# A fused window-attention and gated-conv-FFN kernel: order and PSUM banks from a table, late conv taps on GpSimd and ScalarE, one batch's k transposed by DMA

## The chip, the core and the metric

The kernel runs on one core of a Trainium2 chip. A core has TensorE (PE in the profile: matmuls, with PEld for weight loads), VectorE (DVE), ScalarE (ACT), GpSimd (POOL) and SyncE (SP). SP issues DMAs here and computes nothing. Each engine works through its own list of instructions in order and waits on semaphores for the others. The metric is the device time of one execution in microseconds (us); lower is better.

## What is computed

The reference does attention in a window of 32 positions to either side, then an FFN whose hidden layer is gated by a convolution of 3 taps along the sequence. All inputs and the output are float32.

```python
def _attn_ref(q, k, v):
    B, H, S, D = q.shape                      # 8, 8, 576, 64
    scores = np.matmul(q, k.transpose(0, 1, 3, 2)) / np.sqrt(D)
    mask = np.abs(pos[:, None] - pos[None, :]) <= 32
    scores = np.where(mask, scores, -1000000000.0)
    attn = softmax(scores)
    return np.matmul(attn, v)

def _moe_ref(x, w_in, conv_w, w_out):         # x: (8, 576, 512), d_ff 1024, 3 taps
    h = np.maximum(x @ w_in, 0.0)
    conv_out = sum(conv_w[k] * hp[:, k:k + S, :] for k in range(3))   # hp: h padded by one row
    gate = 1.0 / (1.0 + np.exp(-conv_out))
    return h * gate @ w_out
```

## The kernel before

**Units of work.** Attention runs batch by batch (8), each in two halves of 288 rows (`s` = 0, 1). The FFN runs over the rows of all batches in 12 chunks of 384 (`CH`), so three chunks cover two batches. The first two chunks are cut in two pieces each, so that they can start before a whole batch is there. Within a chunk the hidden width of 1024 is 8 blocks `m` of 128.

**Attention of one half** (`attention`, line 640). `load_qk` (L391) and `load_v` (L422) have SP issue DMAs into float32 staging tiles. `cast_qk`, `cast_v` and `shift_v` turn them into bf16 through the helper `copy` (L301 on ACT, L303 on POOL, L307 on DVE); `shift_v` makes a second copy of v, `vo`, shifted by 64 rows. For batch 0 some of the casts may go to ACT or POOL, later ones go to POOL. `transposes` turns q and k by matmuls with the identity (L491) into PSUM; ACT or DVE copies the result to `qT` and `kT`. `scores` (L541) does the products of 64 rows with 128 keys, exp on ACT (L554) and the mask product (L565; DVE for batches 0 and 1, POOL after that, DVE for the last tile of 64 rows). `values` (L586) multiplies with v and a column of ones; DVE takes the reciprocal (L605) and scales into `xn` (L608). `turn` transposes `xn` into `xT`: by PE (L630) and a copy for batches 0 and 1, by a DMA transpose on SP (L621) for the others.

**FFN of one chunk** (`hidden`, line 662, and `project`, line 788). For each block `m`, four matmuls (L720) give the hidden layer, and ACT writes relu of half of it to `hT` (L736). The convolution is done in PSUM: PE adds a tap by multiplying with a diagonal matrix of the tap's weights (L751), DVE adds a tap by a scalar_tensor_tensor on the bank (L768). The planner's `taps` says which. For chunks 0 and 1 all three taps are PE's; for chunks 2 to 11 they are

```python
        return (1,) if m in TIMES["light"] else (0, 2)     # taps of PE; "light": (1, 2, 3, 7)
```

so that four blocks have one tap on PE and two on DVE, and four have two on PE and one on DVE. Then ACT takes tanh of the bank (L772) and DVE multiplies (1 + tanh) by the hidden value into `gT` (L775). `project` adds 8 matmuls of 512 columns per 128 rows (L795), ACT copies the result to `y_sb` (L806) and SP stores it (L809).

**Weights.** `load_w` brings w_in and w_out in two halves each through the staging tiles `wst`. `conv_weights` builds the 24 diagonals on DVE (L377).

**Order.** None of these calls emits an instruction at once. Each calls `add(on, prio, run, ...)`, which makes an `Op` with the engines it may run on and a cost for each, its due time `prio`, what it reads and writes, and the PSUM bank it takes (`alloc`). Operations are numbered in the order of these calls. `Plan.place` (line 122) is a list scheduler on the host: it keeps the time at which each engine and bank is free, and takes again and again, for the engine that can start first, the ready operation with the earliest due time. It also chooses the engine, where there is a choice, and the bank (one of 8, or a pair). The constants in `TIMES` set due times and how far the planner may reach ahead. At the end the operations are sorted by planned start, warm-up matmuls (`spin`, L817) are put into planned gaps of PE in the first 36 us, and the instructions are emitted in that order. Each engine's order and SP's order of DMAs are therefore fixed when the kernel is built.

The softmax here doesn't subtract the row's maximum and nothing guards it: scores larger than these inputs give would overflow.

## Time and profile before

| | before |
|---|---|
| time, median of 6 executions | 231.18 us (230.91 to 232.88) |
| the profiled execution: time, span | 232.16 us, 230.4 us |
| granted TensorE clock, mean | 0.993 |
| PE busy, matmuls | 213.1 us (92%), 2519 |
| DVE busy | 190.3 us (83%), 416 instructions |
| ACT busy | 171.2 us (74%), 350 |
| POOL busy | 158.1 us (69%), 160 |
| moved by DMA | 45.92 MB, mean 199 GB/s |

A busy time is the time in which an instruction of that engine was in flight, overlaps counted once. Instructions of one engine overlap by their start-up, so the price of one in a packed row is less than its mean duration. A group's row gives line, engine, operation, tiles and shapes, count, then busy time and mean ns of one, then how long the engine stood idle ahead of it and for whom. The slices cut the span in 40 equal parts and give the busy share in tenths (9 is 90% or more). The chain of waits is followed back from the last instruction through what released each step.

### The profile page before, as it was taken

To read this page: it belongs to the slowest core of one execution; us is meant where nothing else is said; L and a number is where in the kernel's file an instruction comes from. 1 tells how busy PE (TensorE), PEld (TensorE's weight loads), DVE (VectorE), ACT (ScalarE), POOL (GpSimd) and SP (SyncE) were. 2 spreads that over 40 slices of the span, in tenths; PEclk is the share of its full clock that TensorE was granted. 3 is DMA by queue.
4 is the path that set the end of the run, shared out by engine and by line. 5 is a ranking of instruction groups with operands and counts; after the bars stand their busy time and mean duration, and the time that the engine had idled before them with its cause. 6 is when DMAs were issued, how large, how long until landed. Compare 5 with 4: busy or idle time off the path is not lost.

```text
span 230.4 us, 6559 instructions
## 1 busy us (share of the span) xinstructions
PE 213.1 (92%) x2519; PEld 130.8 (57%) x2519; DVE 190.3 (83%) x416; ACT 171.2 (74%) x350; POOL 158.1 (69%) x160
## 2 busy tenths in 40 slices
PE   3686999999999997999999988999999999999992
...
DVE  6967467965989889988899977999898988998780
ACT  2384799968576987786988894878878893867642
POOL 6588895989999999986799939886999270000000
...
GB/s 177 289 263 273 278 254 298 327 233 317 279 175 289 101 286 187 267 170 136 251 311 151 270 158 299 137 215 192 291 230 130 127 38 71 91 91 47 89 48 137
DMA packets 68883, 45.92 MB, mean 199 GB/s; under 512 B 53980, under 2 KB 54004, under 8 KB 68852
## 3 DMA queue, kind: packets, MB, share of 16 engines
...
q8 instruction: 19, 0.31, 0.6%
...
q10 hardware_dynamic: 36, 0.01, 0.0%
HBM read 32.52 MB, written 9.44 MB: 182 GB/s over the span
## 4 chain that ended last, share of the span: by engine, by line
PE 64%; POOL 13%; DMA 13%; DVE 3%; SPq 2%; issue 1%; ACT 1%; ACTq 0%; POOLq 0%; DVEq 0%
PE ps_all L720 21%; PE ps_all L795 21%; PE ps_all L751 8%; DMA vst<-in_v_dram 6%; PE ps_all L586 5%; PE ps_all L491 4%; POOL vo L303 4%; DMA wst<-in_moe_w_out_dram 4%; DMA kst<-in_k_dram 3%; PE ps_all L541 3%; POOL attn L565 3%; POOL ve L303 3%; SPq L391 2%; POOL kn L303 2%; POOL qn L303 2%
## 5 line engine op out<-in xcount | busy, mean ns | idle before, releaser
L720 PE MATMUL ps_all<-xT,w_in_sb 128*128 128x385 bf16 (+4 forms) x448 | 77.1, 304 | 0.4 <-DVE xT L307 0.3
L768 DVE SCALAR_TENSOR_TENSOR ps_all<-hT,conv_w_sb,ps_all 128x384 f32<-128x384 bf16 x120 | 70.7, 614 | 6.8 <-PE ps_all L751 5.8
L795 PE MATMUL ps_all<-w_out_sb,gT 128*128 128x512 bf16 x288 | 67.4, 379 | 0.0
L772 ACT ACTIVATE ps_all<-ps_all 128x384 f32<-128x384 f32 (+3 forms) x112 | 49.0, 451 | 13.6 <-DVE ps_all L768 12.4
L775 DVE SCALAR_TENSOR_TENSOR gT<-ps_all,hT 128x384 bf16<-128x384 f32 (+3 forms) x112 | 52.6, 490 | 7.2 <-ACT ps_all L772 5.8
L565 POOL TENSOR_TENSOR attn<-attn,mask 128x1024 bf16<-128x1024 bf16 x24 | 50.9, 2138 | 10.8 <-ACT attn L554 10.7
L736 ACT ACTIVATE hT<-ps_all 128x385 bf16<-128x385 f32 (+4 forms) x112 | 48.6, 462 | 12.0 <-PE ps_all L720 11.1
L720 PEld LDWEIGHTS <-w_in_sb 128*128 128x128 bf16 x448 | 40.5, 98 | 20.6 <-POOL vo L303 0.9
L795 PEld LDWEIGHTS <-gT 128*128 128x128 bf16 x288 | 27.6, 98 | 29.6 <-issue 0.2
L751 PE MATMUL ps_all<-hT,diag_w 128*128 128x384 bf16 (+3 forms) x216 | 43.3, 291 | 0.4 <-DVE gT L775 0.3
L554 ACT ACTIVATE attn<-ps_all 128x1024 bf16<-128x1024 f32 (+1 forms) x40 | 36.4, 950 | 1.1 <-PE ps_all L541 0.5
L303 POOL TENSOR_SCALAR vo<-vst 64x1024 bf16<-64x1024 f32 (+1 forms) x36 | 35.1, 975 | 2.9
L806 ACT COPY y<-ps_all 128x512 f32<-128x512 f32 x36 | 21.1, 593 | 15.5 <-PE ps_all L795 11.4
L608 DVE TENSOR_TENSOR xn<-ps_all,rec 128x256 bf16<-128x256 f32 (+1 forms) x64 | 27.8, 479 | 0.3
L303 POOL TENSOR_SCALAR ve<-vst 128x512 bf16<-128x512 f32 (+1 forms) x41 | 25.5, 631 | 3.3 <-DMA vst<-in_v_dram 2.5
L303 POOL TENSOR_SCALAR kn<-kst 128x1152 bf16<-128x1152 f32 (+1 forms) x20 | 19.7, 987 | 7.8 <-DMA kst<-in_k_dram 7.5
L751 PEld LDWEIGHTS <-diag_w 128*128 128x128 bf16 x216 | 18.1, 97 | 8.0 <-DVE gT L775 0.7
L303 POOL TENSOR_SCALAR qn<-qst 128x1152 bf16<-128x1152 f32 (+1 forms) x20 | 19.3, 967 | 2.5 <-DMA qst<-in_q_dram 1.5
L586 PEld LDWEIGHTS <-attn 128*64 128x64 bf16 x640 | 12.6, 111 | 12.0 <-issue 6.1
L586 PE MATMUL ps_all<-ve,attn 128*64 128x65 bf16 x384 | 15.9, 198 | 2.3 <-DVE attn L565 1.2
L301 ACT COPY qT<-ps_all 128x640 bf16<-128x640 bf16 (+1 forms) x20 | 14.9, 758 | 2.8 <-PE ps_all L491 2.7
L565 DVE TENSOR_TENSOR attn<-attn,mask 128x1024 bf16<-128x1024 bf16 (+1 forms) x16 | 14.4, 918 | 2.7 <-ACT attn L554 2.6
...
## 6 DMA issues: line engine op xcount, KB each, us to landing
...
xT<-xn SPq DMA_TRANSPOSE x30, 3.3
```

Of the source, the lines that this page charges most:

```text
L303: nc.gpsimd.tensor_scalar(out=out_, in0=in_, scalar1=1.0, scalar2=0.0, op0=ALU.mult, op1=ALU.add)
L554: add(act(2 * w), t + 0.1, lambda e: nc.scalar.activation(at, ps(sl, 0, 1024).rearrange("p (e x) -> p e x", e=2)[:, :, 0:w], AF.Exp, bias= ...
L565: lambda e: ENG[e].tensor_tensor(out=x_, in0=x_, in1=m_, op=ALU.mult),
L586: nc.tensor.matmul(ps(sl, lo, lo + D + 1, 64 * j, 64 * j + 64), attn[a][:, 512 * h_ + col:512 * h_ + col + 64], (vo if tt % 2 else ve)[i][ ...
L608: add(dve(2 * n * D), t + 0.1, lambda e, y=y: nc.vector.tensor_tensor(out=xn[i][:, cs[0]:cs[0] + n].rearrange("p c (e g) d -> p c e g d", ...
L720: nc.tensor.matmul(ps(sl, 0, n), w_in_sb[:, kc, m * 128:(m + 1) * 128], x_[:, kc, a0:a1], start=(kc == 0), stop=(kc == KC - 1),)
L736: nc.scalar.activation(o_, i_, AF.Relu, bias=0.0, scale=0.5)
L751: nc.tensor.matmul(ps(sl, 0, no), diag_w[:, kk, m, :], hview(m, o0, o1, kk - 1), start=(kk == ks[0]), stop=(kk == ks[-1]),)
L768: add(("DVE", no / 960.0 + 0.13), tt + 0.1, lambda e, m=m, kk=kk, pv=pv: nc.vector.scalar_tensor_tensor(out=pv(), in0=hview(m, o0, o1, kk ...
L772: add(act(no), tt + 0.2, lambda e, sl=sl: nc.scalar.activation(ps(sl, 0, no), ps(sl, 0, no), AF.Tanh, bias=0.0, scale=1.0), writes=[sl], s ...
L775: add(dve(no), tt + 0.3, lambda e, m=m, mid=mid, i2=i2, pv=pv: nc.vector.scalar_tensor_tensor(out=gT[ig][:, m, o0:o1].rearrange("p (i x) - ...
L795: nc.tensor.matmul(ps(sl, 0, d_model), gT[ig][:, m, 128 * i:128 * i + 128], w_out_sb[:, m, :], start=(m == 0), stop=(m == MB - 1),)
```

## The change

- `Plan.place` no longer searches. `ORDER` lists all 1528 operations by number, `PICK` gives the engine of those that have a choice, `BANKS` the first bank of each operation that takes one, in order. A simple pass still computes planned starts from them.
- `taps` now gives four lists: taps of PE, ACT, DVE and POOL. There are five kinds of block, and the table `kinds` gives each block `m` one, with a row for chunks 2 to 8 and another for chunks 9 to 11. An ACT tap is an activation Copy with the tap's weight as a [128, 1] scale, written to the bank. POOL taps go to the float32 tile `tmp`; a second or third one is added by a POOL tensor_tensor. In kind 3 tanh reads `tmp`; in kind 4 DVE adds `tmp` to the bank.
- k of batch 6 (`"turned": ((6, 1),)`) is no longer loaded in the packed form and transposed by PE: the new `turned` loads it in five blocks of up to 128 rows, casts them on POOL and issues five DMA transposes on SP.
- All casts of batch 0 and of w_in may go to DVE as well (`both`), and batch 0's masks to POOL.
- The last 128 rows are projected in two halves of 256 columns; the second is copied by DVE, and each half has its own store.
- The numbers in `TIMES` are others; with the order taken from the table they have no part in it, apart from the tables named above.

```diff
+ORDER = [
+    73, 80, 0, 1, 2, 25, 17, 3, 10, 21, 26, 15, 29, 36, 27, 34, 30, 37, 47, 48, 20, 8, 51, 52, 28,
+    35, 45, 49, 4, 50, 74, 81, 91, 33, 32, 43, 39, 18, 24, 12, 9, 46, 53, 56, 31, 38, 54, 55, 19,
+    16, 57, 58, 44, 42, 41, 59, 60, 62, 63, 64, 66, 5, 14, 13, 61, 71, 78, 72, 79, 93, 92, 89, 90,
+    94, 95, 96, 97, 98, 65, 69, 67, 100, 70, 103, 104, 125, 129, 126, 40, 6, 128, 68, 239, 235, 101,
+    127, 120, 121, 23, 227, 105, 22, 124, 233, 234, 241, 122, 123, 231, 237, 228, 243, 229, 99, 76,
...
+    1521, 1522, 1523, 1517, 1518, 1519, 1524, 1525, 1526, 1527,
+]
+PICK = {
+    34: "POOL", 35: "POOL", 36: "POOL", 37: "DVE", 38: "DVE", 39: "DVE", 40: "POOL", 41: "ACT",
+    42: "POOL", 43: "POOL", 44: "POOL", 46: "ACT", 48: "ACT", 50: "DVE", 52: "DVE", 55: "DVE",
+    58: "DVE", 68: "DVE", 70: "ACT", 78: "ACT", 79: "ACT", 80: "POOL", 81: "ACT", 82: "DVE",
+    83: "DVE", 84: "DVE", 85: "POOL", 86: "POOL", 87: "POOL", 88: "POOL", 90: "ACT", 92: "ACT",
+    94: "DVE", 96: "ACT", 99: "DVE", 102: "DVE", 105: "DVE", 115: "ACT", 117: "DVE", 119: "DVE",
+    121: "DVE", 122: "POOL", 123: "POOL", 124: "POOL", 126: "POOL", 127: "ACT", 128: "POOL",
...
+BANKS = [
+    3, 0, 3, 0, 3, 4, 0, 2, 0, 2, 6, 5, 4, 4, 0, 6, 2, 4, 6, 0, 5, 4, 1, 3, 2, 5, 4, 0, 1, 6, 4, 5,
...
-    "light": (1, 2, 3, 7),
+    "kinds": ((2, 2, 4, 3, 2, 4, 0, 1), (1, 2, 0, 2, 0, 0, 2, 2), (3, 1, 4, 2, 3, 2, 2, 1)),
+    "turns": (2, 9),
+    "turned": ((6, 1),),
...
+        order, banks = [self.ops[i] for i in ORDER], iter(BANKS)
+        assert sorted(ORDER) == list(range(len(self.ops)))
+        for op in order:
+            e = op.eng = PICK.get(op.idx) or next(iter(op.on))
+            r = max([d.end for d in op.deps], default=0.0)
+            if op.alloc is not None:
+                n = op.alloc.n
+                x = next(banks)
+                r = max(bank[x:x + n] + [r])
+                assert r < 1e9, "no bank is free"
+                op.alloc.base = x
+                bank[x:x + n] = [1e9] * n
+            f = free[e]
+            if e == "PE":
+                f += self.SWITCH * (op.mode != mode)
+                mode = op.mode
+                r += self.LATE * (r > f)
+            op.start = max(r, f)
+            f = free[e] = op.start + op.on[e]
...
+    def both(n):
+
+        return ("DVE", n / 1920.0 + 0.2)
...
-        on = dict([act(n), pool(n)]) if (b, s) == (0, 0) else pool(n)
+        on = dict([act(n), pool(n), both(n)]) if b == 0 else pool(n)
...
-        on = dict([act(n), pool(n)]) if b == 0 and p1 <= 128 and c < 3 and p0 < 64 else pool(n)
+        on = dict([act(n), pool(n), both(n)]) if b == 0 else pool(n)
...
+    def turned(b, y, s):
+
+        i = b % NLD
+        src = (q, k)[y][b]
+        a0, a1, a2 = TIMES["ahead_t"]
+        for c in ((0, 1, 2), (3, 4))[s]:
+            t = when(b, s, 0.0) + 0.1 * c + 0.01 * y
+            p = min(128, S - 128 * c)
+            st_ = wst[y].rearrange("p (c h d) -> p c h d", c=4, h=H)[:, c] if c < 4 else rest[64 * y:64 * y + 64]
+            to = n2[y][:, c] if c < 4 else n2r
+            nk = ("n2", y, c) if c < 4 else "n2r"
+            key = ("rest", y) if c == 4 else ("wst", y, c)
+            add(sp(1.1), t - a0, lambda e, c=c, p=p, st_=st_: nc.sync.dma_start(
+                st_[0:p], src[:, 128 * c:128 * c + p, :].rearrange("h p d -> p h d")
+            ), writes=[key], dma=0.0112 * p, rel=t - a0)
+            add(pool(H * D), t - a1, lambda e, p=p, st_=st_, to=to: copy(
+                e, to[0:p].rearrange("p g e d -> p e g d"), st_[0:p].rearrange("p (e g) d -> p e g d", e=2)
+            ), reads=[key], writes=[nk])
+            lo = 128 * c + PAD * y
+            add(sp(1.26), t - a2, lambda e, p=p, lo=lo, to=to: nc.sync.dma_start_transpose(
+                out=(qT, kT)[y][i][:, :, lo:lo + p], in_=to[0:p].rearrange("p g e d -> p (g e d)")
+            ), reads=[nk], writes=[("Tc", y, i, c)], dma=0.0051 * p)
+
...
+            if (b, y) in TIMES["turned"]:
+                continue
...
+    KINDS = (
+        ((0, 2), (), (1,), ()), ((1,), (), (0, 2), ()), ((), (1,), (0, 2), ()), ((), (), (), (1, 0, 2)),
+        ((1,), (), (), (0, 2)),
+    )
+
     def taps(c, m):

         if c < 2:
-            return TIMES["taps"][c]
-        return (1,) if m in TIMES["light"] else (0, 2)
+            return TIMES["taps"][c], (), tuple(k_ for k_ in range(3) if k_ not in TIMES["taps"][c]), ()
+        return KINDS[TIMES["kinds"][(c >= TIMES["turns"][0]) + (c >= TIMES["turns"][1])][m]]
...
+            by_pe, by_act, by_dve, by_pool = taps(c, m)
+
+            def mm(e, m=m, sl=sl, ks=by_pe):
                 for kk in ks:
                     nc.tensor.matmul(
                         ps(sl, 0, no), diag_w[:, kk, m, :], hview(m, o0, o1, kk - 1),
                     )

             tt = t + (m + TIMES["lag"][0]) * dt
-            add(pe(no, len(taps(c, m))), tt, mm, reads=hk + [("diag", kk, m) for kk in taps(c, m)], writes=[sl], alloc=sl,
-                slots=[sl], group=gr)
+            if by_pe:
+                add(pe(no, len(by_pe)), tt, mm, reads=hk + [("diag", kk, m) for kk in by_pe], writes=[sl],
+                    alloc=sl, slots=[sl], group=gr)
             mid = hview(m, o0, o1, 0)
             i2 = mid.shape[1]

             def pv(sl=sl, i2=i2):
                 return ps(sl, 0, no).rearrange("p (i x) -> p i x", i=i2)

-            for kk in (0, 1, 2):
-                if kk in taps(c, m):
-                    continue
+            for kk in by_act:
+                add(("ACT", 0.000833 * no + 0.18), tt, lambda e, m=m, kk=kk, pv=pv: nc.scalar.activation(
+                    pv(), hview(m, o0, o1, kk - 1), AF.Copy, bias=0.0, scale=conv_w_sb[:, kk, m:m + 1],
+                ), reads=hk + ["conv_w"], writes=[sl], alloc=sl, slots=[sl], group=gr)
+            if by_pool:
+                r = NTM[0] % len(tmp)
+                NTM[0] += 1
+
+                def tv(x=0, r=r, i2=i2):
+                    return tmp[r][:, x, 0:no].rearrange("p (i x) -> p i x", i=i2)
+
+            for n_, kk in enumerate(by_pool):
+                add(pool(no), tt + 0.05, lambda e, m=m, kk=kk, tv=tv, n_=n_: nc.gpsimd.tensor_scalar(
+                    out=tv(n_ > 0), in0=hview(m, o0, o1, kk - 1), scalar1=conv_w_sb[:, kk, m:m + 1], scalar2=0.0,
+                    op0=ALU.mult, op1=ALU.add,
+                ), reads=hk + ["conv_w"], writes=[("tmp", r, n_ > 0)])
+                if n_:
+                    add(("POOL", 0.0021 * no + 0.155), tt + 0.05, lambda e, tv=tv: nc.gpsimd.tensor_tensor(
+                        out=tv(), in0=tv(), in1=tv(1), op=ALU.add,
+                    ), reads=[("tmp", r, True)], writes=[("tmp", r, False)])
+            if by_pool and by_pe:
+                add(("DVE", no / 960.0 + 0.13), tt + 0.1, lambda e, pv=pv, tv=tv: nc.vector.scalar_tensor_tensor(
+                    out=pv(), in0=tv(), scalar=1.0, in1=pv(), op0=ALU.mult, op1=ALU.add,
+                ), reads=[("tmp", r, False)], writes=[sl], slots=[sl], group=gr)
+            for kk in by_dve:
                 add(("DVE", no / 960.0 + 0.13), tt + 0.1, lambda e, m=m, kk=kk, pv=pv: nc.vector.scalar_tensor_tensor(
                     out=pv(), in0=hview(m, o0, o1, kk - 1), scalar=conv_w_sb[:, kk, m:m + 1], in1=pv(),
                     op0=ALU.mult, op1=ALU.add,
                 ), reads=hk + ["conv_w"], writes=[sl], slots=[sl], group=gr)
-            add(act(no), tt + 0.2, lambda e, sl=sl: nc.scalar.activation(
-                ps(sl, 0, no), ps(sl, 0, no), AF.Tanh, bias=0.0, scale=1.0
-            ), writes=[sl], slots=[sl], group=gr)
+            if by_pool and not by_pe:
+                add(act(no), tt + 0.2, lambda e, pv=pv, tv=tv: nc.scalar.activation(
+                    pv(), tv(), AF.Tanh, bias=0.0, scale=1.0
+                ), reads=[("tmp", r, False)], writes=[sl], alloc=sl, slots=[sl], group=gr)
+            else:
+                add(act(no), tt + 0.2, lambda e, sl=sl: nc.scalar.activation(
+                    ps(sl, 0, no), ps(sl, 0, no), AF.Tanh, bias=0.0, scale=1.0
+                ), writes=[sl], slots=[sl], group=gr)
...
-        for m0, m1 in ((0, 6), (6, MB)) if c == NCH - 1 else ((0, MB),):
-            def mm(e, m0=m0, m1=m1):
-                for m in range(m0, m1):
-                    nc.tensor.matmul(
-                        ps(sl, 0, d_model), gT[ig][:, m, 128 * i:128 * i + 128], w_out_sb[:, m, :],
-                        start=(m == 0), stop=(m == MB - 1),
-                    )
-
-            add(pe(d_model, m1 - m0), t + m0, mm,
-                reads=[("gT", ig, m, (i, x)) for m in range(m0, m1) for x in (False, True)]
-                + [("w_out", m) for m in range(m0, m1)],
-                writes=[sl], alloc=None if m0 else sl, slots=[sl], group=gr if m1 == MB else None)
         r = NYY[0] % NY
         NYY[0] += 1
-        add(act(d_model), t + 0.1, lambda e: nc.scalar.copy(out=y_sb[r], in_=ps(sl, 0, d_model)),
-            reads=[sl], writes=[("y", r)], slots=[sl], group=gr)
         r0 = c * CH + 128 * i
-        add(sp(), t + 0.2, lambda e: nc.sync.dma_start(out_rows[r0:r0 + 128, :], y_sb[r]),
-            reads=[("y", r)], dma=0.8)
+        end = c == NCH - 1 and i == 2
+        for f0, f1 in ((0, d_model // 2), (d_model // 2, d_model)) if end else ((0, d_model),):
+            for m0, m1 in ((0, 6), (6, MB)) if c == NCH - 1 else ((0, MB),):
+                def mm(e, m0=m0, m1=m1, f0=f0, f1=f1):
+                    for m in range(m0, m1):
+                        nc.tensor.matmul(
+                            ps(sl, f0, f1), gT[ig][:, m, 128 * i:128 * i + 128], w_out_sb[:, m, f0:f1],
+                            start=(m == 0), stop=(m == MB - 1),
+                        )
+
+                add(pe(f1 - f0, m1 - m0), t + m0, mm,
+                    reads=[("gT", ig, m, (i, x)) for m in range(m0, m1) for x in (False, True)]
+                    + [("w_out", m) for m in range(m0, m1)] + [(sl, 0)] * (f0 > 0),
+                    writes=[(sl, f0)], alloc=None if m0 or f0 else sl, slots=[sl],
+                    group=gr if m1 == MB and not end else None)
+            on = act(f1 - f0)
+            if end and f0:
+                on = dve(f1 - f0)
+            add(on, t + 0.1, lambda e, f0=f0, f1=f1: copy(e, y_sb[r][:, f0:f1], ps(sl, f0, f1)),
+                reads=[(sl, f0)], writes=[("y", r, f0)], slots=[sl], group=None if end else gr)
+            add(sp(), t + 0.2, lambda e, f0=f0, f1=f1: nc.sync.dma_start(
+                out_rows[r0:r0 + 128, f0:f1], y_sb[r][:, f0:f1]
+            ), reads=[("y", r, f0)], dma=0.8 * (f1 - f0) / d_model)
```

## The prediction

> **What bounds the kernel now.** I read the page's busy shares first, then its slices, then the busy time by stage, then the chain of waits in one stage, then the groups.
>
> The page, busy times and slices:
>
> ```profile
> PE 213.1 (92%) x2519; PEld 130.8 (57%) x2519; DVE 190.3 (83%) x416; ACT 171.2 (74%) x350; POOL 158.1 (69%) x160
> ...
> PE   3686999999999997999999988999999999999992
> ...
> DVE  6967467965989889988899977999898988998780
> ACT  2384799968576987786988894878878893867642
> POOL 6588895989999999986799939886999270000000
> ```
>
> PE is full from the fifth slice to the last but one; POOL is busy up to 80% of the span and then does nothing. Busy time by stage (columns: length, PE, PEld, DVE, ACT, POOL with their counts, clock, DMA share, GB/s):
>
> ```profile
> 0.00:40.00 40.00, 31.20 (x443) 23.05 (x443) 28.50 (x85) 26.77 (x64) 29.25 (x48) 0.96 1.00 262
> ...
> 65.00:182.00 117.00, 113.62 (x1368) 66.66 (x1366) 104.74 (x215) 94.14 (x180) 101.16 (x86) 1.00 0.88 209
> 182.00:226.00 44.00, 44.00 (x316) 23.27 (x313) 37.64 (x73) 30.21 (x64) 4.20 (x2) 1.00 0.21 70
> ...
> 150.00:160.00 10.00, 10.00 (x124) 5.78 (x123) 9.71 (x21) 7.77 (x17) 8.09 (x7) 1.00 0.84 223
> ```
>
> From 65 to 182 us chunks 2 to 8 run beside the attention of batches 2 to 7; from 182 to 226 us it is chunks 9 to 11. PE has 157.6 of these 161 us. The chain of waits from 100 to 125 us is PE alone, and its pieces give PE's true prices (a matmul's own mean of 327 ns is mostly pipeline):
>
> ```profile
> by line: PE ps_all L795 35.0%; PE ps_all L720 32.7%; PE ps_all L751 12.4%; PE ps_all L491 8.5%; PE ps_all L586 6.5%; PE ps_all L541 5.5%
> ...
> 105.04 0.78 PE ps_all L491 x14
> ...
> 109.65 0.33 PE ps_all L751 x2
> 110.96 1.73 PE ps_all L795 x8
> ```
>
> So a tap (one diagonal matmul of the conv, L751, 384 columns) costs 0.163 us, a transpose (L491) 0.056. Prices of the others, from the groups by shape:
>
> ```profile
> L768 DVE SCALAR_TENSOR_TENSOR ps_all<-hT,conv_w_sb,ps_all 128x384 f32<-128x384 bf16 x120 | 70.7, 614 | 6.8 <-PE ps_all L751 5.8
> L565 POOL TENSOR_TENSOR attn<-attn,mask 128x1024 bf16<-128x1024 bf16 x24 | 50.9, 2138 | 10.8 <-ACT attn L554 10.7
> ...
> L772 ACT ACTIVATE ps_all<-ps_all 128x384 f32<-128x384 f32 x80 | 39.0, 494 | 13.1 <-DVE ps_all L768 12.4
> ...
> L303 POOL TENSOR_SCALAR ve<-vst 128x512 bf16<-128x512 f32 x39 | 24.3, 632 | 3.3 <-DMA vst<-in_v_dram 2.5 <-POOL vo L303 0.3
> ```
>
> **The conv, part by part.** Before, chunks 2 to 11 have 12 taps on PE and 12 on DVE each. The row of `kinds` for chunks 2 to 8 has three blocks of kind 0 (PE 2, DVE 1), one of kind 1 (PE 1, DVE 2), four of kind 2 (ACT 1, DVE 2): PE 7, DVE 13, ACT 4. For chunks 9 to 11: PE 3, DVE 10 and one add, ACT 3, POOL 8 taps and 5 sums.
> - PE: 7x5 + 3x9 = 62 taps less, 62 x 0.163 = 10.1 us, all on the path.
> - DVE: 7x1 - 3x1 = 4 more, at 70.7/120 = 0.59: +2.4 us.
> - ACT: 37 taps. The nearest row is the tanh of the same size: 494 ns, and two in a row take 0.86 (195.73 us), so 0.38 each when packed: 14.1 us. That tanh has immediate operands; these taps read their scale from a [128,1] column, which no ACT instruction of this trace does. The Trainium skill (ScalarE: Activation LUTs, "What ACT_TABLE_LOAD costs") says such an operand adds about 93 ns: 0.47 each, 17.5 us by estimate. This speaks against the change by 3.4 us of ACT. I take 17.5; ACT is not the largest, so the sum moves by nothing, but every tap stands that much later before its DVE taps.
> - POOL: from 632 ns at 512 and about 1180 at 1152 elements, a 384-element tap is 0.52; a sum of two tensors lies between 0.80 (2138 x 384/1024) and 2.14, taken as 0.9. 24 x 0.52 + 15 x 0.9 = 26 us, where POOL has 4.2 of 44 us: hidden, unless a block's chain (3 taps, 2 sums, 3.4 us) starts late. The table puts them behind batch 7's last mask, and PE still has chunk 8's projections and chunk 10's hidden layer (10 us) meanwhile. Without that cover the price is the 3.4 us, once. DVE's taps read one SBUF operand and last 614 ns both beside a busy POOL (90 to 170 us) and an idle one (615 after 187 us), so I charge no contention.
>
> **Order and banks.** The planner's search runs on the host; reading a table costs the chip nothing. What the new order itself does to each queue no row can price: the gain is bounded by PE's idle time (4.4 us from 40 to 226 us), the loss by nothing, and I put 0 for it, with a rival on either side. Banks matter as waits of PE for a reader's end; PE shows hardly any today (0.3 us of L751 for DVE's gT).
>
> **k of batch 6.** Less: 18 transposes (1.0 us PE), four copies of about 0.76 us (by the table's choices ACT has 35 of such copies instead of 39, DVE 25 as before), two POOL casts of 1.2, four loads. More: five loads, five DMA transposes, five casts of 0.63 (POOL +0.8 us). On SP's queue the loads take 0.6 each and a transpose 1.25 (L621's row): +7 us of issue, and a transpose that waits for its cast holds every load and store behind it. The table issues the loads two to three chunks ahead, and batch 6 is needed only near 150 us, so I cost it at 0 to +2, taking 0.
>
> **Stage 65 to 226 us (161 us).** PE 157.6 - 11.1 = 146.5; DVE 142.4 + 2.4 = 144.8; ACT 124.4 + 17.5 - 3 = 139; POOL 105.4 + 0.8 + 26 = 132. PE stays the largest by 2 us only. At its present 98% the stage would be 149.7 (gain 11.3); DVE would then have to be busy 97%. The row of 150 to 160 us shows both so full (10.00 and 9.71), but it is the best of its kind; DVE's mean is 88%. I take 95.5% for PE: 153.4, **gain 7.6**. At 91% the gain is gone.
>
> **The start.** Before, the first hidden matmul waits at 23.34 for this chain:
>
> ```profile
> 6.01 6.85 DMA vst<-in_v_dram
> ...
> 18.04 0.95 POOL vo L303
> ...
> 23.34 1.47 PE ps_all L720 x12
> ```
>
> Seven casts of v lie one after the other on POOL from 13.0 to 19.0. Numbering the operations as `add` is called (0 to 2 conv weights, 3 to 26 diagonals, 27 to 33 the first loads, 34 to 44 the casts), `PICK` sends 38 and 39 to DVE, 41 to ACT; `ORDER` puts 40 after 42 to 44. Three casts are left before the first values: 3.4 us earlier. v's loads stand behind six loads, not eight (2 x 0.64): 1.3 us. But w_in's first half lands at 18.44 with the DMA share at 1.18 in 10 to 20 us, and its place behind these loads is the same: no hidden matmul before some 19.1 + a cast, 20. That bounds the gain at 3.5 us. Against it: eight casts go to DVE. The trace has one DVE operation of that sort beside POOL, the mask:
>
> ```profile
> L565 DVE TENSOR_TENSOR attn<-attn,mask x16: 418/758/2184, 14.0 to 189.5; 128x1024 bf16<-128x1024 bf16 x8, 128x512 bf16<-128x512 bf16 x8
> ```
>
> 418 ns with POOL idle (189.5 us), up to 2184 with it busy. The skill (SBUF — State Buffer, "Who interferes with whom") says that a fast DVE copy or cast takes the port pair that DVE and POOL share for its whole length, and one waits for the other. At the planner's own 0.47 eight casts cost 3.8 us; with a POOL cast waited for (0.47 + 0.63), 8.8. DVE has 8.2 us free in the first 30. Taking 1.0 each I leave **2.3 us** of the 3.5 (range -1 to 3.5).
>
> **The end.** The last projection comes in halves, its second copied by DVE (0.41 us, as xn's 128x256) instead of ACT's 0.59, with a store half as large after it. Of the 4.0 us from the last matmul on: **0.4** (0.2 to 0.8).
>
> Sum: 7.6 + 2.3 + 0.4 = 10.3. The profiled execution took 232.16 (span 230.4); 221.9, and against the median of 231.18, in proportion, **220.9 us**.
>
> **Rivals.**
> - *DVE and ACT become the bound and nothing is gained from 65 to 182 us.* For: DVE at 90% there already, +3.7 us of taps (7 x 0.53). Then only chunks 9 to 11 (27 taps, 4.4 us, less 0.4), start and end give: 231.2 - 6.7 = 224.5, to 229.
> - *The table also closes gaps:* PE keeps its 98% (11.3 instead of 7.6), the start gains 3.5, and the first 40 us, where PE lies idle 8.8 and turns over 21 warm-up matmuls for 8.3, give 3 more: 231.2 - 18.2 = 213.
> - *Slower: DVE waits for ACT's taps.* Now:
>
> ```profile
> ACT ps_all L772 <- DVE ps_all L768: 12.4, 23, 1.1
> ...
> DVE ps_all L768 <- PE ps_all L751: 5.8, 18, 0.9
> ```
>
> A tap on DVE then waits for relu, ACT's tap and the hand-over, ACT's tap may stand behind an exp of 1.03 us, and behind the waiting DVE stand gT and xn, for which PE's projections and values wait. DVE would need 144.8, plus its idle time of 18.6 less the 11.1 by which PE comes sooner, plus x for the waits: 152.3 + x against 161 + 2.7 of start and end. It decides at x = 11.4, 0.31 us for each of 37 taps. At ACT's present 0.54 (12.4/23) for every one, x = 20: 239 us. At the present frequency (18 waits in 80 blocks) it is 4.5, within my 95.5%.
> - *The change doesn't do what it says*: the counts of L751 or of PE's transposes would be as before. The table's length and kinds leave little room.
>
> **Numbers.** The likeliest case 0.64 (216 to 225.5); limit on DVE and ACT 0.15; gaps closed too 0.07; within 0.5% (about what a measurement tells from no change) 0.03; slower 0.11. Faster 0.86. The range 212.5 to 228.5 leaves out the slower and equal cases and the ends of the two others.
>
> **What would show it.** PE's conv matmuls of 384 columns 58, not 120; transposes 270, not 288; 37 new ACT instructions near 0.47 packed and 0.59 alone; POOL busy 26 us more after batch 7's masks; the first hidden matmul near 21 us; PE at 95% in the stage that was 161 us. If DVE's waits on ACT's taps pass 11 us, or SP's transposes of k delay loads of batches 6 and 7 so that PE waits near 150 us, I am wrong.

## The result, and the profile after

The changed kernel takes 229.27 us (median of 16 runs, 227.01 to 230.91); the kernel before, timed beside it, 231.36 (37 runs). The ratio is 0.9883, with a 95% interval of 0.9859 to 0.9907: 2.7 us gained, where 10.3 were forecast, and above the forecast range of 212.5 to 228.5. Executions of one kernel fall into faster and slower ones, and every ratio here compares the faster ones alone, which is why 2.7 us is more than the difference of the two medians; the profiled execution of the changed kernel is a slower one (230.69 us, span 229.0), so the profile of e7 below, which differs only in its output buffers (226.84 us, span 225.1), is set beside it where sizes matter.

The page, for busy times and slices:

```profile
PE 203.6 (89%) x2445; PEld 125.3 (55%) x2445; DVE 197.7 (86%) x431; ACT 184.6 (81%) x381; POOL 183.7 (80%) x194
...
PE   4677588989889979999999899959899999999994
...
DVE  7487799658999997899998999958699999999980
ACT  2278468998759898979999998949999986999872
POOL 6233796999989996999996999565999999999910
...
DMA  5999899998986979989859988999799402522233
```

PE's row, nearly full before from the fifth slice on, now has 8s, 7s and a 5 in it up to slice 29. POOL's seven empty slices at the end are filled, but for the last two. The row that matters is the last one: the 16 DMA engines are mostly at 8 to 9 tenths until slice 31. That was so before too, and the prediction made nothing of it. The same row before:

```profile
DMA  5999999999989499974899999487974412321213
```

Busy time by stage of the changed kernel (columns as before: length, PE, PEld, DVE, ACT, POOL, clock, DMA share, GB/s):

```profile
0.00:40.00 40.00, 27.38 (x375) 19.52 (x376) 31.24 (x88) 23.38 (x49) 22.05 (x36) 1.00 0.94 261
...
65.00:182.00 117.00, 110.46 (x1372) 64.75 (x1370) 106.76 (x221) 104.15 (x202) 102.02 (x90) 1.00 0.91 213
182.00:226.00 44.00, 43.40 (x319) 23.23 (x316) 39.86 (x82) 36.65 (x80) 35.39 (x44) 1.00 0.31 101
150.00:160.00 10.00, 7.59 (x68) 4.25 (x69) 7.03 (x14) 6.71 (x16) 5.61 (x7) 1.00 1.03 241
```

In the stretch 150 to 160 us, which was full of PE's work before, each of the four engines is now idle for 24 to 44% of the time, while the DMA share is 1.03 (0.84 before). Part of this hole is a wait of ACT for an output buffer (3.1 us ahead of its copy at 153.2 us), which e7 does not have. In e7 the row is

```profile
150.00:160.00 10.00, 9.08 (x116) 4.79 (x113) 7.37 (x13) 8.25 (x16) 6.05 (x7) 1.00 0.96 231
```

so PE is idle for 9% and the other three for 18 to 40%. Where no engine is full, the cause may lie outside the engines.

The groups by shape show that the parts of the change do what they say:

```profile
L868 PE MATMUL ps_all<-hT,diag_w 128*128 128x384 bf16 x58 | 15.4, 327 | 0.2 <-ACT hT L852 0.2
L908 DVE SCALAR_TENSOR_TENSOR ps_all<-hT,conv_w_sb,ps_all 128x384 f32<-128x384 bf16 x121 | 70.4, 615 | 2.6 <-PE ps_all L868 1.1 <-ACT ps_all L884 0.4 <-PE ps_all L644 0.2
L917 ACT ACTIVATE ps_all<-ps_all 128x384 f32<-128x384 f32 x74 | 34.9, 490 | 3.8 <-DVE ps_all L908 3.4
L884 ACT ACTIVATE ps_all<-hT,conv_w_sb 128x384 f32<-128x384 bf16 x37 | 21.8, 590 | 0.5
L900 POOL TENSOR_TENSOR tmp<-tmp 128x384 f32<-128x384 f32 x15 | 14.8, 996 | 0.7
L895 POOL TENSOR_SCALAR tmp<-hT,conv_w_sb 128x384 f32<-128x384 bf16 x24 | 13.8, 586 | 0.4
```

58 taps on PE (the line of the taps is now L868), 37 on ACT, 24 taps and 15 sums on POOL, and DVE (L908) waits for ACT's taps for 0.4 us in all. PE lost its work (its busy time on the page is 9.5 us less, matmuls overlapping), and it is a smaller part of the chain that ended last. Before, by engine:

```profile
PE 64%; POOL 13%; DMA 13%; DVE 3%; SPq 2%; issue 1%; ACT 1%; ACTq 0%; POOLq 0%; DVEq 0%
```

and after:

```profile
PE 43%; DVE 17%; DMA 11%; POOL 11%; ACT 7%; issue 5%; SPq 5%; ACTq 0%; POOLq 0%; DVEq 0%
```

In e7 PE has 49%. The share of DMA in the chain is no larger than before, so the chain alone does not name the cause.

PE's waits can be counted from the trace: the time from one matmul's start to the next, less what a matmul of that size takes when packed (0.22 us at 512 columns), summed where more than 0.06 us is left. Gaps ahead of projections are left out, because some traces lack records of projections. In the first 40 us, the wait for the first matmul included, they are 16.8 us before and 20.1 after; from 40 to 185 us 13.2 before and 19.3 after. (The expectations below count from 40 us to the end, with those ahead of projections: 14.0 before, 20.9 after.) Of the 11.1 us that the change took from PE, 9.4 came back as waits (about 7 in e7).

The places of chunk 2 and chunk 9 in the trace (start of the first hidden matmul, us) divide the span more sharply than fixed windows. They were read for every kernel; these are the ones that the argument needs:

| kernel | chunk 2 | chunk 9 | chunks 2 to 8 take | last matmul | span |
|---|---|---|---|---|---|
| before | 64.4 | 181.6 | 117.2 | 226.0 | 230.4 |
| changed | 67.3 | 183.6 | 116.3 | 225.5 | 229.0 |
| e7, five output buffers | 64.5 | 179.7 | 115.2 | 221.7 | 225.1 |
| e11, three engines relieved | 62.1 | 177.9 | 115.8 | 219.7 | 223.2 |
| e12, PE relieved by 10 us | 65.4 | 182.1 | 116.7 | 224.1 | 227.5 |
| e17, before with half loads | 64.3 | 179.4 | 115.1 | 223.8 | 228.3 |
| e13, changed with half loads | 65.2 | 174.6 | 109.4 | 216.6 | 220.0 |
| e14, e11 and half loads | 64.5 | 172.8 | 108.3 | 214.6 | 218.0 |

In these rows the middle takes 115 to 117 us whatever is done to the engines, and 108 to 109 where the changed kernel's loads are halved. (The gain of e11 lies ahead of chunk 2. In e5 below the middle takes 113.2 us, but chunk 2 starts at 67.4, after a stretch in which PE lies idle.) How that was found, misses included, is the next section.

### The profile page after: what moved, and what is told of

Same layout as the page of the kernel before. It is cut to its first block, busy times and chain, and to the rows that moved or that the text cites. A ratio compares the mean times of both kernels' runs of the same rounds, so it can differ in the third digit from the quotient of the medians.

```text
span 229.0 us, 6466 instructions
## 1 busy us (share of the span) xinstructions
PE 203.6 (89%) x2445; PEld 125.3 (55%) x2445; DVE 197.7 (86%) x431; ACT 184.6 (81%) x381; POOL 183.7 (80%) x194
## 2 busy tenths in 40 slices
DMA packets 75603, 46.51 MB, mean 203 GB/s; under 512 B 61084, under 2 KB 61364, under 8 KB 75572
## 4 chain that ended last, share of the span: by engine, by line
PE 43%; DVE 17%; DMA 11%; POOL 11%; ACT 7%; issue 5%; SPq 5%; ACTq 0%; POOLq 0%; DVEq 0%
PE ps_all L836 16%; PE ps_all L945 15%; DMA wst<-in_moe_w_in_dram 5%; POOL attn L672 5%; DMA vst<-in_v_dram 4%; SPq L469 4%; DVE attn L672 4%; PE ps_all L868 4%; PE ps_all L693 3%; DVE ps_all L908 3%; DVE xn L715 3%; DVE gT L920 3%; POOL vo L381 3%; ACT ps_all L917 2%; PE ps_all L644 2%
## 5 line engine op out<-in xcount | busy, mean ns | idle before, releaser
L836 PE MATMUL ps_all<-xT,w_in_sb 128*128 128x385 bf16 (+4 forms) x448 | 75.0, 305 | 7.6 <-ACT y L379 1.8
L908 DVE SCALAR_TENSOR_TENSOR ps_all<-hT,conv_w_sb,ps_all 128x384 f32<-128x384 bf16 x121 | 70.4, 615 | 2.6 <-PE ps_all L868 1.1
L945 PE MATMUL ps_all<-w_out_sb,gT 128*128 128x512 bf16 (+1 forms) x296 | 67.8, 373 | 0.1
L852 ACT ACTIVATE hT<-ps_all 128x385 bf16<-128x385 f32 (+4 forms) x112 | 46.6, 453 | 6.8 <-PE ps_all L836 6.1
L917 ACT ACTIVATE ps_all<-ps_all 128x384 f32<-128x384 f32 (+3 forms) x106 | 44.2, 439 | 7.6 <-PE ps_all L868 3.5
L945 PEld LDWEIGHTS <-gT 128*128 128x128 bf16 x296 | 28.1, 98 | 28.7 <-issue 0.4
L379 ACT COPY y<-ps_all 128x512 f32<-128x512 f32 (+1 forms) x36 | 21.0, 589 | 10.9 <-PE ps_all L945 7.6
L868 PE MATMUL ps_all<-hT,diag_w 128*128 128x384 bf16 (+3 forms) x154 | 26.3, 276 | 1.1 <-DVE gT L920 0.9
L381 POOL TENSOR_SCALAR ve<-vst 128x512 bf16<-128x512 f32 (+1 forms) x36 | 23.7, 664 | 4.0 <-DMA vst<-in_v_dram 3.2
L884 ACT ACTIVATE ps_all<-hT,conv_w_sb 128x384 f32<-128x384 bf16 x37 | 21.8, 590 | 0.5
L379 ACT COPY kT<-ps_all 128x640 bf16<-128x640 bf16 (+1 forms) x19 | 14.2, 754 | 7.8 <-PE ps_all L594 7.7
L381 POOL TENSOR_SCALAR kn<-kst 128x1152 bf16<-128x1152 f32 (+1 forms) x16 | 16.0, 1002 | 4.8 <-DMA kst<-in_k_dram 4.6
## 6 DMA issues: line engine op xcount, KB each, us to landing
wst<-in_moe_w_in_dram SPq DMA_DIRECT2D x2, 1024.0 KB, 10.6
```

Of the source, the lines that this page charges most:

```text
L381: nc.gpsimd.tensor_scalar(out=out_, in0=in_, scalar1=1.0, scalar2=0.0, op0=ALU.mult, op1=ALU.add)
L836: nc.tensor.matmul(ps(sl, 0, n), w_in_sb[:, kc, m * 128:(m + 1) * 128], x_[:, kc, a0:a1], start=(kc == 0), stop=(kc == KC - 1),)
L852: nc.scalar.activation(o_, i_, AF.Relu, bias=0.0, scale=0.5)
L868: nc.tensor.matmul(ps(sl, 0, no), diag_w[:, kk, m, :], hview(m, o0, o1, kk - 1), start=(kk == ks[0]), stop=(kk == ks[-1]),)
L908: add(("DVE", no / 960.0 + 0.13), tt + 0.1, lambda e, m=m, kk=kk, pv=pv: nc.vector.scalar_tensor_tensor(out=pv(), in0=hview(m, o0, o1, kk ...
L917: add(act(no), tt + 0.2, lambda e, sl=sl: nc.scalar.activation(ps(sl, 0, no), ps(sl, 0, no), AF.Tanh, bias=0.0, scale=1.0), writes=[sl], s ...
```

## The experiments

Theories at first: A, the table's order loses what the lighter conv gains; B, the start loses it; C, DVE, second in load, has become the bound; D, stores or the turned k disturb the middle. Each ratio below is to the kernel before, on the same chip; the changed kernel stands at 0.9883, and a gain over it is the difference of the two ratios, times 231 us. (Some expectations compare medians instead; they say 7.9 us where the ratios give 7.0, and 3.8 for 2.9.) Kernels e6, e9 to e15, e17 and e18 leave out part of the work or of the data, to time the rest.

**e1, e2, e3: parts of the change in the planner's order.** The kernel before with the changed kernel's kinds of blocks, its own search for the order kept:

```diff
 e1 (chunks 9 to 11 alone)
-    "light": (1, 2, 3, 7),
+    "kinds": ((0,1,1,1,0,0,0,1), (0,1,1,1,0,0,0,1), (3,1,4,2,3,2,2,1)),
 e2 (chunks 2 to 8 alone)
+    "kinds": ((0,1,1,1,0,0,0,1), (1,2,0,2,0,0,2,2), (0,1,1,1,0,0,0,1)),
 e3 (all parts of the change except the table of order, engines and banks)
```

> The kernel before, in its planner's order, with one part of the change alone: the kinds of block of chunks 9 to 11 (PE 3 taps, DVE 10 and an add, ACT 3, POOL 8 taps and 5 sums each). Theory A (the new order of the queues loses what the new conv gains): the conv part is as priced, 27 taps of 0.163 less 0.4: about 3.6 us faster than before, 227.7. Theory B (with ACT and DVE near full the engines miss each other, whatever the order): in this stage ACT has 30 of 44 us and POOL 4, so a good part is gained here too, 2 to 3.6 us. Below 1 us gained both are wrong for this stage.

> The kernel before, in its planner's order, with the kinds of block of chunks 2 to 8 alone (PE 7, DVE 13, ACT 4 taps for 12 and 12). Theory A: PE's 5.7 us less show by more than half: 3 to 5 us faster than before, 227 to 228. Theory B: no gain or a loss, 230.5 to 234, with DVE and ACT each above 90% of the stage from chunk 2 to chunk 9 and PE waiting longer.

> All parts of the change (both rows of kinds, batch 6's k by DMA, batch 0's casts also on DVE, the halved end), but order, engines and banks chosen by the planner of before with its constants instead of the tables. Only the order differs from the changed kernel. Theory A: 221 to 225, clearly below the changed kernel's 229.3. Theory B: 228 to 231, like the changed kernel.

Measured: e1 230.52, ratio 0.9932 [0.9905, 0.9959]; e2 235.15, 1.0138 [1.0078, 1.0197]; e3 242.69, 1.0426 [1.0366, 1.0486]. Theory A finds no support: with the same operations the planner's order is 12.6 us slower than the table's (its costs and due times were tuned for other work, so that isn't the best a planner could do). The late chunks alone gave 1.6 us of the 3.6 expected, and the middle kinds alone lost 3.2.

**e4: v's last loads ahead of the second of w_in's two loads in the table.** In the trace of the changed kernel, SP issues both halves of w_in (2 MB) and then sits on two loads of v (columns: start, us):

```profile
11.06 1.14 SPq L540 DMA_DIRECT2D wst<-in_moe_w_in_dram  x2
12.25 7.13 SPq L500 DMA_DIRECT2D vst<-in_v_dram  x2
```

and the chain of waits in its first 40 us goes through w_in's landing and the casts that follow on DVE, v's among them:

```profile
11.70 12.51 DMA wst<-in_moe_w_in_dram
24.24 0.43 DVE w_in_sb L385
...
26.63 1.51 DVE ve L385 x2
```

```diff
 ORDER: operations 76, 77, 75 (loads of batch 0's last v blocks)
-  ... 74, 81, 91, ... 120, 121 (w_in) ... 76 ... 77 ... 75
+  ... 76, 77, 75, 120 (w_in) ...
```

> The changed kernel with three numbers of its table moved: the loads of the second half of batch 0's v (75, 76, 77) ahead of the load of w_in's first half (120). In the changed kernel both halves of w_in go first, v of the second half is cast only from 26.6 us on, and the second piece of chunk 0 starts at 37.1 us instead of 32.2. Theory A with this as its main place: that piece starts near 33 to 34 us and 2 to 3 us remain at the end: 226 to 227. Theory B, or a start that later waits absorb: 228.5 to 229.5.

Measured: 231.33, 0.9958 [0.9932, 0.9983]. v comes sooner, w_in later, and the second piece of chunk 0 starts at 38.2 us instead of 37.1. In these 40 us the DMA share is 0.98 (0.94 in the changed kernel, 1.00 before), so the order of two transfers mostly decides which of them is late; this version is 1.7 us slower than the changed kernel.

**e5: the start of the kernel before.** The 296 operations that the planner of before issues in its first 40 us come first, in its order, with its engines and banks; the rest follows in the table's order.

> The changed kernel with the first part of its table replaced: the 296 operations that the planner of before plans ahead of 40 us (batches 0 and 1, pieces of chunks 0 and 1, their loads) come first, in the planner's order with its engines and banks; all others follow in the table's order. The first 40 us are then those of before. Theory S (the start cost the change 4 to 5 us at the second piece of chunk 0, and that goes through to the end): chunk 0's second piece again near 32 us, the end 3 to 4 us earlier than the changed kernel, 225 to 226. Theory C (what is gained at the start is lost again at the next engine that is full, as GpSimd is from 45 to 85 us): 228 to 230.

Measured: 0.9927 [0.9862, 0.9992] (12 runs from 227.71 to 235.31, median 232.63; the ratio rests on three of them). The start is back (second piece of chunk 0 at 32.1 us, as before), but PE lies idle for 4.2 us where the two orders meet, and chunk 2 starts at 67.4, chunk 9 at 180.6. Not faster than the changed kernel: Theory B doesn't explain the loss alone.

**e6, e7, e8: DVE, the stores, the turned k.**

```diff
 e6
-  out=pv(), in0=hview(m, o0, o1, kk - 1), ... in1=pv(),
+  out=pv()[:, :, 0:256 // i2], in0=hview(m, o0, o1, kk - 1)[:, :, 0:256 // i2], ... in1=pv()[:, :, 0:256 // i2],
 e7
-  NY = 3
+  NY = 5
-  n2 = [pp.tile(...) for n in "qk"]
+  n2 = [None, pp.tile(...)]
 e8 (ORDER, PICK and BANKS adapted to PE's transposes of this batch)
-    "turned": ((6, 1),),
+    "turned": (),
```

> The changed kernel with DVE's 121 taps over 256 of 384 columns (the conv of the other third lacks these taps), so each about 0.13 us shorter, 16 us of DVE in all, nearly all of it from chunk 2 on. Theory C (PE waits since DVE, ACT and POOL are all near full): the time falls by 4 us or more, to 225 or less. Theory D (loads, stores and transposes on SP's queue come late, whatever the engines do): less than 1.5 us.

> The changed kernel with five output tiles y instead of three (the unused half of n2 makes room). In its profile ACT's copy to y waited 3.1 us at 150 us for a store that stood behind k's and xn's transposes on SP's queue. Theory D: that wait is gone and 1.5 to 3 us with it, 226.5 to 228. Theory C: the wait only moves, 228.5 to 229.5.

> The changed kernel with k of batch 6 loaded in the packed form, cast once per half and transposed by PE again (18 matmuls and 4 copies, put into the table behind q's; 5 loads of small packets, 5 casts and 5 DMA transposes less). Theory D: SP is free of 7 us of issue between 120 and 155 us, 1.5 to 3 us faster, 226 to 228. Theory C: PE and ACT get 1.0 and 3 us more: 229 to 231.

Measured: e6 228.06, 0.9844 [0.9797, 0.9891]; e7 229.21, 0.9881 [0.9842, 0.992]; e8 228.88, 0.9886 [0.9841, 0.9931]. 16 us less on DVE gave 0.9 us, and its interval overlaps the changed kernel's; buffers and the turned k gave nothing. C falls, and so does D as far as buffers and the turned k go. (e8 also spares SP's queue: the durations of its issues from 40 to 165 us add up to 95.6 us, for 102.7 in the changed kernel and 94.6 before. Queue time alone is not what the loss is.) PE's waits from 40 to 185 us stay at 18.7 to 19.0 in all three.

New theories: C', POOL's masks and casts set the pace; E, ACT does; F, a fixed order is bound by its hand-offs, no engine by itself; G, the engines are joint bounds and each relief is taken by the next.

**e9 to e12: each engine relieved, then three together, then PE.**

```diff
 e9
+            if e == "POOL":
+                x_, m_ = x_[:, :, 0:128], m_[:, :, 0:128]
 e10
-  ps(sl, 0, no), ps(sl, 0, no), AF.Tanh
+  ps(sl, 0, no // 2), ps(sl, 0, no // 2), AF.Tanh
 e11 = e6 + e9 + e10
 e12
-  for m in range(m0, m1):
+  for m in range(m0, m1 - 2 * (c < 8)):
```

> The changed kernel with GpSimd's mask multiply over half of its elements (24 instructions of 2.12 us; the other half of the weights stays unmasked): about 24 us less on GpSimd, of which the page shows 183.7 busy, nothing else touched. Theory C' (GpSimd's masks and casts, 9.6 of 10 busy between 45 and 190 us, set the pace and make TensorE wait): 5 us or more off, 224 or less, ratio 0.967, with TensorE's waits after 40 us down from 20.9 to 15 or less. Theory F (what TensorE waits for is the hand-offs of a fixed order, each with another engine last; no single engine sets the pace): at most 1.5 us off, 228 to 229, waits near 20.

> The changed kernel with ScalarE's tanh over half of its columns (the other half of the sum goes on without tanh): 74 instructions fall from 0.49 to about 0.32 us, the small ones by less, about 14 us less on ScalarE, of which the page shows 184.6 busy; the chain from conv to tanh to product gets shorter by 0.17 us a block too. Theory E (ScalarE sets the pace): 4 us or more off, 225 or less, ratio 0.972. Theory F: at most 1.5 us off, 228 to 229, waits of TensorE after 40 us near 20.

> The changed kernel with all three reliefs together: VectorE's taps over two thirds of their columns (about 16 us), tanh over half (14 us), the masks on GpSimd over half (24 us). TensorE has its work as it was. Theory G (each of the three engines is nearly full, and relieving one only hands the wait to the next): 6 us or more off, 223 or less, ratio 0.963, with TensorE's waits after 40 us falling from 20.9 to 14 or less. Theory F in its strict form (order and latency of hand-offs alone, whatever the load): no more than 2 us off, 227 to 229, waits 18 or more.

> The changed kernel with TensorE's own work cut: the projections of chunks 0 to 7 sum six of eight blocks of 128 hidden units (two blocks are left out), 48 matmuls of 512 columns fewer, at about 0.215 us each 10.3 us less of TensorE between 50 and 185 us; no other engine's work changes. If TensorE's load still sets the pace in that stage: 7 to 10 us off, 219 to 222, ratio 0.96. If the other engines set it (theories C', E, G): 0 to 3 us off, 226 to 229, ratio 0.98, and TensorE's waits after 40 us grow from 20.9 to 28 or more.

Measured:

| run | us | ratio | PE's waits 40 to 185 |
|---|---|---|---|
| e9 | 228.69 | 0.9842 [0.9755, 0.9929] | 17.4 |
| e10 | 230.88 | 0.9961 [0.9929, 0.9993] | 20.3 |
| e11 | 225.45 | 0.9756 [0.9694, 0.9818] | 17.2 |
| e12 | 228.85 | 0.9913 [0.9879, 0.9946] | 29.6 |

No relief of one engine gave a gain that its interval tells from the changed kernel, so C' and E fall; with half of tanh away the kernel even came out 1.8 us slower, for which no cause was found. All three together, some 50 us of work, gave 2.9 us, where G wanted 6 or more and strict F no more than 2: neither. And e12 is the sharpest: 10.3 us taken from PE gave nothing, and PE's waits rose by as much (29.6 us for 19.3). So PE was not the bound of the changed kernel's middle, and the other three explain little of it. What to try next came from POOL's waits in e11, from 40 to 190 us (columns: us in total, times, longest):

```profile
POOL qn L381 <- DMA qst<-in_q_dram: 10.4, 6, 2.6
POOL kn L381 <- DMA kst<-in_k_dram: 7.6, 4, 3.0
POOL ve L381 <- DMA vst<-in_v_dram: 5.3, 4, 2.0
POOL qn L381 <- DMA kst<-in_k_dram: 3.0, 1, 3.0
POOL vo L381 <- DMA vst<-in_v_dram: 1.8, 3, 1.0
```

POOL, given 24 us, spends 28.1 waiting for q, k and v to arrive. The same view of the kernel before:

```profile
POOL attn L565 <- ACT attn L554: 10.7, 6, 4.0
POOL kn L303 <- DMA kst<-in_k_dram: 4.3, 2, 3.5
POOL ve L303 <- DMA vst<-in_v_dram: 1.6, 3, 0.8
```

and of the changed one:

```profile
POOL kn L381 <- DMA kst<-in_k_dram: 3.5, 2, 1.9
POOL ve L381 <- DMA vst<-in_v_dram: 3.2, 3, 1.6
POOL qn L381 <- DMA qst<-in_q_dram: 2.6, 1, 2.6
POOL attn L672 <- ACT attn L657: 1.3, 2, 1.1
POOL vo L381 <- DMA vst<-in_v_dram: 1.3, 1, 1.3
```

Before, POOL mostly waited for the other engines (10.7 us for exp), and 5.9 for loads. After, it is 1.3 for exp and 10.6 for loads (1.2 and 10.0 in e7), as if the engines had got ahead of the DMA stream. This sign is not a proof: e8, at the changed kernel's time, has 7.1 for exp and 4.2 for loads, close to the picture before. And the busy time from 40 to 165 us, with the DMA share in the column before the last, of the kernel before, of the changed one and of e12:

```profile
40.00:165.00 125.00, 120.56 (x1555) 74.30 (x1553) 108.33 (x225) 99.54 (x198) 109.83 (x98) 1.00 0.94 228
40.00:165.00 125.00, 115.83 (x1546) 72.56 (x1545) 109.93 (x227) 108.19 (x224) 109.66 (x103) 1.00 0.93 224
40.00:165.00 125.00, 110.02 (x1516) 69.49 (x1513) 113.35 (x230) 108.02 (x223) 109.80 (x100) 1.00 0.99 223
```

The DMA engines are 0.93 to 0.99 busy there, at 223 to 228 GB/s. Relieving PE raised the share to 0.99, but not the rate. So Theory H: the arrival of the loads paces chunks 2 to 8.

**e13 to e16.**

```diff
 e13 (loads of q and k; v likewise with half of its heads)
-  st[y][s][:, h_]...,                   [[RP * D, 32], [S * D, NP], [1, RP * D]]
+  st[y][s][:, h_]...[:, 0:RP * D // 2], [[RP * D, 32], [S * D, NP], [1, RP * D // 2]]    # b > 1
 e14 = e11 + e13
 e15 = e11 + e12
 e16 = e7 + the planner's operations of its first 30 us put first, as in e5
```

> The changed kernel with the loads of q, k and v of batches 2 to 7 cut to half of their bytes (the other half of each staging buffer keeps an older batch's values), about 13 of the 46.5 MB that the page counts; every instruction on the engines stays. The DMA engines are 0.93 busy between 40 and 165 us. Theory H (arrival of the loads paces the middle, through GpSimd's casts): 4 us or more off, 225 or less, ratio 0.972, and GpSimd's waits for q, k and v after 65 us, 10.6 us in the profile, nearly gone. Theories F and G: at most 1.5 us off, 228 to 229.

> The three reliefs of VectorE, ScalarE and GpSimd together (225.45) with the loads of batches 2 to 7 cut to half as well; TensorE's work as it was. Theory H, or H and G together: 220 or less, ratio 0.952, TensorE's waits after 40 us 10 or less. Theory F (order and latency): 224 to 226, ratio 0.974, waits 14 to 18.

> The three reliefs together (225.45, 3.8 us below the changed kernel) and TensorE's cut of 10.3 us (alone 0 to 1 us) in one kernel. Theory G (TensorE and the three engines are joint bounds in one fixed order, so that a cut on one side alone is taken by the other): more than the sum of the two, 7 to 12 us below the changed kernel, 217 to 222, ratio 0.95. If something else paces (H: loads; F: latencies of the order): no more than the sum, 224 to 226, ratio 0.973.

> The changed kernel with five output buffers, and the instructions that the planner of before issues in its first 30 us put first, in its order and with its banks; everything after them in the table's order. The start is then that of before to 30 us (second piece of chunk 0 near 33 us, 37.1 in the changed kernel's profile), and the seam comes before the one at 40 us that cost 4.2 us. If the start is a separate loss: 225 to 227, ratio 0.977. If the seam, or GpSimd's and ScalarE's work further on, takes it back: 228 to 230, ratio 0.988.

Measured:

| run | us | ratio | PE's waits 40 to 185 |
|---|---|---|---|
| e13 | 221.34 | 0.9581 [0.9536, 0.9625] | 13.1 |
| e14 | 219.15 | 0.9488 [0.9443, 0.9533] | 10.3 |
| e15 | 225.22 | 0.9716 [0.9637, 0.9794] | 27.8 |
| e16 | 233.10 | 1.0077 [1.0042, 1.0111] | 21.8 |

e13 alone, with every engine's work as it was, is 7.0 us faster than the changed kernel. Its page counts 36.48 MB for 46.51, 10 MB less (the expectation's 13 was too high). A load of q, k or v now lands 3.1 to 3.4 us after its issue (medians from 40 to 165 us), for 4.3 to 5.0 in the changed kernel. POOL's waits from 40 to 190 us are turned over:

```profile
POOL attn L672 <- ACT attn L657: 3.9, 6, 1.2
POOL qn L381 <- PE ps_all L868: 1.7, 1, 1.7
POOL ve L381 <- DMA vst<-in_v_dram: 0.6, 1, 0.6
```

and the stretch of 150 to 160 us is full again, with the DMA share at 0.68:

```profile
150.00:160.00 10.00, 9.84 (x159) 5.92 (x161) 8.36 (x19) 9.75 (x18) 9.11 (x7) 1.00 0.68 180
```

e15 agrees from the other side: PE's cut on top of the other three's gives at most 0.9 us more (0.9716 against 0.9756, intervals overlapping), where Theory G wanted more than the sum, so the joint bound of the engines was not it. e14 leaves only 2.2 us to the three reliefs once the loads are light. e16, the attempt at a better version, is slower than the kernel before; its start did not become the earlier one that was hoped for (second piece of chunk 0 at 37.4 us, 33 expected), so it says nothing on what the start is worth.

**e17, e18: was it so before, and is it bandwidth?** The cut of e13 in the kernel before, and in the changed kernel the stores of chunks 0 to 7 instead:

```diff
 e18
-  out_rows[r0:r0 + 128, f0:f1], y_sb[r][:, f0:f1]
+  out_rows[r0:r0 + 128, f0:f0 + 128], y_sb[r][:, f0:f0 + 128]    # c < 8
```

> The kernel before with the same cut of the loads of q, k and v of batches 2 to 7 to half of their bytes; its order of instructions unchanged. In the changed kernel that cut took 7.9 us (221.34 after 229.27). If the DMA engines paced the kernel before just as much (theory H for both): 223 to 225, ratio 0.968, and the change is worth 2 to 3 us with or without them. If TensorE paced it (as the prediction read the profile, with waits of 14 us after 40 us) and the change moved the bound to the loads: 229 to 231, ratio 0.995, and the change would be worth 8 to 9 us under light loads, about what was predicted.

> The changed kernel with the stores of the output rows of chunks 0 to 7 cut to a quarter of their columns: 4.7 MB fewer of 46.5 MB between 56 and 176 us, on no path of its own (five buffers in the place of three gave nothing). If it is the bandwidth of the DMA engines that stores and loads share: 13 MB fewer gave 7.9 us, so 2 to 4 us off, 225 to 227, ratio 0.98. If it is the latency of the loads alone, or their place in the order: at most 1 us off, 228.5 to 229.5, ratio 0.99.

Measured: e17 230.26, 0.9952 [0.9913, 0.9992]; e18 226.52, 0.9786 [0.9739, 0.9833]. In the kernel before, half the bytes are worth 1.1 us, in the changed one 7.0. With full loads the change gains 2.7 us; with halved loads on both sides 8.6 (0.9581/0.9952 = 0.963; the two intervals together make it 0.957 to 0.969). So before, the loads just kept up and the removal of PE's work was still worth something; the change made PE's part shorter and the arrival of the loads took over. The DMA share of e17 from 40 to 165 us,

```profile
40.00:165.00 125.00, 122.34 (x1583) 76.67 (x1595) 111.93 (x232) 102.21 (x206) 112.47 (x99) 1.00 0.57 153
```

falls from 0.94 to 0.57 with next to no gain, which is what a resource that is nearly full but not limiting looks like. e18 speaks for the shared stream: 4.7 MB less of stores, on no path of their own (e7 gave their buffers more room for nothing), are worth 2.2 us, 0.5 us per MB beside 0.7 per MB of loads. It rests on four runs, but its interval lies clear of the changed kernel's.

Of the versions that leave out nothing none was faster than the changed kernel (e7, e8: the same; e5: not told from it; e4 and e16: slower).

## Why the prediction was wrong

**What held.** The counts (58, 37, 24 and 15 instructions, 270 transposes). The prices: an ACT tap 0.59 us as foreseen for one alone, 0.10 over the tanh (0.49) where the Trainium skill's page "ScalarE: Activation LUTs" (What ACT_TABLE_LOAD costs) gives about 0.093 for the pointer operand (the tanh reads PSUM and the tap SBUF, so the 0.10 need not be the operand's alone); POOL's share 28.6 us (13.8 + 14.8) for 26, hidden as said. The first hidden matmul at 21.9 for 21. The late stage: from chunk 9's start to the last matmul 41.9 us for 44.4, so 2.5 gained; 95.5% of PE after 27 taps less gives the same (44.0 - 4.4 = 39.6, 39.6/0.955 = 41.5, by estimate). The DMA share is 0.31 there. The end 1.0 for 0.4, above its range (from the last matmul's start, 4.4 us before and 3.4 after). The third rival, DVE waiting for ACT's taps, came to 0.4 us of the 11.4 at which it would have decided.

**Step one that failed: the stage of 161 us, 7.6 us.** "PE stays the largest by 2 us only", and 95.5% was chosen for PE. The list had PE, DVE, ACT and POOL; the DMA engines were not in it, though their share stood in the lines that were shown (0.88 from 65 to 182 us) and is 0.94 from 40 to 165. From chunk 2's start to the last matmul the kernel before takes 161.6 us, the changed one 158.2 and e7 157.2: a gain of 3.4 to 4.4. With halved loads it is 159.5 against 151.4: 8.1, near the forecast's 7.6. Chunks 2 to 8 are where it went wrong: at 95.5% of PE they should have given 5.0 ((113.6 - 6.7)/0.955 = 112.0 for 117, by estimate); they give 5.7 with light loads (115.1 to 109.4) and 0.9 to 2.0 with full ones. What the change takes from PE and gives to the others was read rightly; the arrival of the loads, a term of the sum that was put at nothing without a reason, was not. (One tap on DVE is priced at 0.59 us in the sum and at 0.53 in the first rival; neither changes the outcome.)

**Step two that failed: the start, 2.3 us.** The first hidden matmul is 1.4 us earlier, but the second piece of chunk 0 starts at 37.1 us (32.2 before), and chunk 2 at 67.3 for 64.4; in e7 it is 34.3 and 64.5. So the start is worth -2.9 to -0.1, not +2.3. The prediction said that w_in's first half bounded the start and looked no further: the second half is now ahead of v's last loads of batch 0, which land at 25.1, 26.4 and 28.0 us (19.2, 20.3 and 22.8 before), and the chain goes through w_in's landing and v's casts. The feared price of DVE's casts came to less: the eight took 4.85 us in all, not 8.0. The three that started just ahead of a cast on POOL (12.74, 19.78 and 24.24 us) took 0.43, and POOL's cast took 0.78 to 0.85, for 0.61 to 0.62 where no cast of DVE ran beside it (13.71 and 21.23 us); those that started under one took 0.8 (1.59 for two at 26.55 us); the other two met no cast on POOL, but for the last 0.04 us of one. That fits the shared port pair that the skill's page "SBUF — State Buffer" (Who interferes with whom) describes, where whoever issues first holds the pair; POOL lost 0.16 to 0.24 us of the 0.30 to 0.38 for which DVE's cast was still running. On the chain the start waits 12.5 us for w_in, in a DMA stream that is nearly full (0.94; 1.01 in e7), and then for casts and other work that has gathered on DVE. e4 and e5 moved it without gaining, so what the start alone would be worth is not settled.

**The rivals.** The nearest in time was the first (224.5 to 229), and its mechanism is refuted: e6 and e10 show that neither DVE nor ACT was the bound, and in e11, with both and POOL relieved, chunks 2 to 8 still take 115.8 us. "SP's transposes of k delay loads ... so that PE waits near 150 us" named the right place: PE is busy 7.59 of 10 us there (9.08 in e7). But without the turned k (e8) the time is the same, while fewer bytes on the same issues (e13) bring PE back to 9.84.

**What the runs leave open.** Which loads matter most. v's and the transposes' packets are small (the page counts 61084 of 75603 packets under 512 B), and it wasn't tried whether longer packets would do what fewer bytes did: halving v took away 13824 of these packets together with the bytes (47260 are left in e13). Only e18 took bytes and left as many packets (75603). The page "Perfetto Trace Analysis" (What "DMA-bound" means) names among its limits the 16 DMA engines and the sequencer that issues. Here the engines' share of 0.93 to 0.99 and e18 speak for the first. e13 does not decide, since with fewer bytes SP's issues get shorter too (91.2 us for 102.7, from 40 to 165 us); e8, which saves 7 us of issue and gains nothing, speaks against the second. Nor was it tried to give q, k and v a second staging tile. SP's loads stood 15.4 us (40 to 190 us) until POOL had emptied the tile that they write, for 5.9 before; in e13 they stood 14.7 and the kernel was fast, so this alone is not the cause, but it may be part of how the loads come late. In e8 it is 18.0, and e8's loads were not halved.
